# Phi of the first two query tiles of the last quarter, second attention: three operations on ScalarE and one on VectorE in place of one and two

## The chip, the cores and the metric

The kernel runs on one core of a Trainium2 chip. The metric is device time in microseconds (us) of one execution; lower is better. Engines are named as the profile names them: PE is TensorE's matmul, PEld its weight load, DVE is VectorE, ACT is ScalarE, POOL is GpSimd, and SPq is the queue of SyncE, which issues nearly all DMAs. Each engine takes its own instructions strictly in order; an instruction that waits for another engine holds up all that stands behind it on its engine.

## The reference

The network has four layers on x of shape 2048 x 1024: linear attention (A), gated ReGLU block (B), and the same two again with the same weights. What matters here is the attention:

```
qkv = layernorm(x) @ wqkv                       # 32 heads of 32
phi = lambda t: where(t > 0, t + 1, exp(t)) + 1e-6
pq, pk = phi(q), phi(k)
kv  = einsum("bhsd,bhse->bhde", pk, v);   z = sum over s of pk
o   = (pq @ kv) / ((pq . z) + 1e-6)
x   = x + o.reshape(B, S, D) @ wo
```

Phi is computed as max(t, 0) + (min(exp(t), 1) + 1e-6), or, which is the same in value, as max(t, 0) + (exp(-max(-t, 0)) + 1e-6).

## The kernel before

The 2048 rows are 16 tiles of 128 rows; four tiles are a quarter (`sc` or `q`, 0 to 3; `j` is the tile in its quarter). The 1024 columns are two halves of 512 (`c` or `n2`, 0 and 1). A tile's half is a unit: eight matmuls of 128 x 512 into one PSUM bank. `l` is 0 in the first attention and 2 in the second, so `l and ...` is true in the second alone.

An attention layer runs in this order: keys and queries of quarters 0 to 2 in turn (`k_unit`, `q_unit`), the keys of quarter 3, then the product of normalised x and phi(k) (`m_products`, L534), from which `kv` comes (`kv_half`, L485), and then the queries of quarter 3, the output units and the folding of `wo`.

**Queries of quarter 3.** `q_unit(sc, j, c)` projects (`project`, L436) and takes phi of the PSUM bank `ps` into half `c` of tile `pq`. `phi` has two kinds:

```
if kind == "v":
    nc.scalar.activation(out=e, in_=ps, func=ACT.Exp)                          # L375
else:
    nc.scalar.activation(out=e, in_=ps, func=ACT.Relu, scale=-1.0)             # L377
    nc.scalar.activation(out=e, in_=e, func=ACT.Exp, scale=-1.0)               # L378
    nc.scalar.activation(out=e, in_=e, func=ACT.Identity, bias=self.eps6[:, 0:1])   # L379
...
if kind == "v":
    nc.vector.tensor_scalar(out=e, in0=e, scalar1=1.0, scalar2=1e-6, op0=ALU.min, op1=ALU.add)  # L383
nc.vector.scalar_tensor_tensor(out=out, in0=ps, scalar=0.0, in1=e, op0=ALU.max, op1=ALU.add)    # L385
```

Before, queries of quarters 0 to 2 take kind "s", those of quarter 3 kind "v"; keys always take "v". L383 reads and writes float32 in SBUF; L385 reads `ps` from PSUM and `e` from SBUF and is the last reader of the bank.

**Folding.** `finish_kv` copies the two banks of `kv` to SBUF, one with DVE (L588) and one with ACT (L589). `fold_wo(n)`, n = 0 to 3, multiplies 16 small blocks of it by `wo` (PE, L641) into four PSUM banks, of which DVE copies one (L650) and ACT three (L648) into `T`. All four calls use the same four banks (`kv0`, `kv1` of one pool, two of `ps3`), so a fold's first matmul waits until the copies of the fold ahead are done.

**The order on PE** in this stretch of the second attention is: query unit (0,0); the last part of `kv`; units (0,1), (1,0); fold 0; units (1,1), (2,0); fold 1; units (2,1), (3,0); fold 2; unit (3,1), first output unit (L656); fold 3; the other output units, each added to x by DVE (L663).

**Denominators.** For each of the 16 query tiles `z_mult` (POOL, L610) multiplies pq by z into `kvc`, `z_sum` (DVE, L615 to L617) sums and inverts, `z_scale` (POOL, L622) scales pq, and a DMA transpose on SPq (L627) brings it to `pqT`, the operand of the output units. These chains for tiles 0 to 10 are under way while PE computes the last queries.

**What sets the order.** Tasks are put off by a count of units (`later.at`, one tick each unit). In this stretch the orders of DVE and POOL are those in which the program issues (`manual_schedule`), so DVE's queue holds L383 and L385 of the units, L588, L650 and the denominators' L615 to L617 interleaved; the order of ACT is the framework's. SPq issues, in order: transposes of pqT, the two halves of `wo` (L37), x rows 0 to 7 back from DRAM (L230), and the first weights of the next layer (L778, L781).

**After it.** The output units of the later quarters run beside the layer norm of the next layer: DVE statistics (L154, L159), ACT scaling (L188), DMA transposes to xnT (L352), and the sums of xnT on DVE (L823 to L826) which the next layer's first matmuls (L850) read.

Of the kernel before, what the change touches and what calls it, by code (L numbers as in the profile page):

```python
# [15 lines left out]
NW = 512  # L16
# [73 lines left out]
class _Net:  # L90
# [318 lines left out]
    def layer_A(self, l, last_ln):  # L409
# [18 lines left out]
        def project(name, l_q, j, between=None):  # L428
            w = ring.get((l, name))

            spare = l_q < self.NQ - 1 and next(turns) % 3 == 2
            ps = (self.ps3 if spare else self.ps).tile([P, NW], F32, tag="b" if spare else "a")
            for kt in range(KT):
                if between and kt == KT - 2:
                    between()
                nc.tensor.matmul(by_row(ps), lhsT=self.xnT[l, l_q][:, kt, j * P:(j + 1) * P],  # L436
                                 rhs=w[:, kt, :].rearrange("p (b i d) -> p i b d", i=R, d=HD),
                                 start=(kt == 0), stop=(kt == KT - 1))
            return ps
# [153 lines left out]
        def q_unit(sc, j, c, lag=None):  # L593
            if c == 0 and (sc, j) not in pq_of:
                a = self.slot(f"pq{l}_{sc}", [P, QT, D])
                for i in range(QT):
                    pq_of[sc, i] = a[:, i, :]
            pq = pq_of[sc, j]
            self.phi(project(f"q{c}", sc, j), pq[:, c * NW:(c + 1) * NW], "s" if sc < self.NQ - 1 else "v")
            if c == H - 1 and lag is not None:  # L600
                later.at(lag, lambda: z_mult(sc, j))

# [5 lines left out]
        def z_mult(sc, j):  # L608
            prod = ksum
            nc.gpsimd.tensor_tensor(out=prod, in0=pq_of[sc, j], in1=zrow, op=ALU.mult)  # L610
            later.at(2, lambda: z_sum(prod, sc, j))
# [79 lines left out]
        if l == 0:  # L691
            first = self.head_units(lambda *a: k_unit(0, *a), lambda *a: q_unit(0, *a), *steps)
        else:
            first = column_major(k_unit, 0)
# [6 lines left out]
        if l == 0:  # L701
            with self.tc.manual_schedule(engines={mybir.EngineType.DVE, mybir.EngineType.SP,
                                                  mybir.EngineType.Activation}):
                quarter0()
        else:
            run(first, column_major(q_unit, 0))
        for q in range(1, self.NQ - 1):
            if (l, q) == (0, 1):
                for i in range(self.U // 2):
                    later.at(1 + 8 * i, lambda i=i: self.make_d(2 * i))  # L710
            run(row_major(k_unit, q), row_major(q_unit, q))
# [351 lines left out]
```

## Time and profile before

| | us |
|---|---|
| median of 5 runs | 1486.56 |
| lowest to highest | 1484.92 to 1489.65 |
| profiled execution | 1486.11 |
| its span, first to last instruction | 1484.2 |
| PE busy in the span | 1471.7 (99%) |
| DVE busy | 872.9 (59%) |
| ACT busy | 513.1 (35%) |
| POOL busy | 283.8 (19%) |
| PE busy from 893 to 917 us | 20.36 of 24.00 |

The span is read in microseconds from its start. In the timeline a line is start, length, engine, code line, operation, out<-in, with the idle time ahead of it and what ended that in brackets; consecutive instructions of one kind are merged with a count. A matmul's length has its pipeline's tail in it, so that the next may start before its end. In the list of waits a line is who waited for whom: total, times, longest. The last queries of the second attention and the four folds lie between 893 and 917 us; the first matmul of the next layer starts at 972.93 us.

### The profile page before, as it was taken

How to read it: one execution, taken by the hardware profiler on the slowest of the kernel's cores; microseconds unless marked ns; L12 is line 12 of the kernel's file. 1: busy time of each engine (PE TensorE's matmuls, PEld its weight loads, DVE VectorE, ACT ScalarE, POOL GpSimd, SP SyncE). 2: the span in 40 equal slices, each digit the busy share in tenths (PEclk: the TensorE clock that was granted, in tenths of full speed). 3: DMA queues.
4: the chain of work that ended last, by engine and by line, in shares of the span. 5: the costliest groups of instructions: out<-in, count | busy, mean ns of one | idle time of the engine just before them, and what ended most of it. 6: DMA issues, size and time to landing. Idle time of an engine off the chain costs nothing.

```text
span 1484.2 us, 18646 instructions
## 1 busy us (share of the span) xinstructions
PE 1471.7 (99%) x7007; PEld 668.2 (45%) x7007; DVE 872.9 (59%) x1495; ACT 513.1 (35%) x919; POOL 283.8 (19%) x190
## 2 busy tenths in 40 slices
PE   9999999999999999999999999999999999999999
PEld 4444444444444444444444444444444444444444
DVE  8995787666594434455379767873445433434632
ACT  5752323333330333340067423343333203333300
POOL 1356540111100011110023484401111000111000
PEclk9999999999999999999999999999999999999999
DMA  9855438444458954435833029894444688444461
GB/s 280 226 164 175 114 60 245 156 142 157 160 187 252 339 175 132 149 128 195 255 99 71 1 41 291 211 279 142 137 147 131 186 245 269 142 142 147 149 208 43
DMA packets 316059, 251.32 MB, mean 169 GB/s; under 512 B 105536, under 2 KB 291136, under 8 KB 315072
## 3 DMA queue, kind: packets, MB, share of 16 engines
q1 hardware_dynamic: 306000, 229.80, 52.7%
q10 hardware_dynamic: 9968, 20.32, 3.6%
q8 instruction: 55, 0.90, 0.3%
q14 instruction: 36, 0.29, 0.1%
HBM read 190.84 MB, written 34.60 MB: 152 GB/s over the span
## 4 chain that ended last, share of the span: by engine, by line
PE 90%; DVE 6%; POOL 2%; DMA 1%; issue 1%; ACT 0%; SPq 0%; DVEq 0%
PE ps L436 14%; PE yg L850 10%; PE dy L934 10%; PE yu L850 10%; PE dv L934 7%; PE dx L934 7%; PE xu L850 6%; PE xg L850 6%; PE ps L473 4%; PE vg L850 3%; PE vu L850 3%; PE zu L850 3%; PE zg L850 3%; PE ps L656 2%; DVE x L663 1%; DVE stats L154 1%
## 5 line engine op out<-in xcount | busy, mean ns | idle before, releaser
L850 PEld LDWEIGHTS <-w 128*128 128x128 f16 (+1 forms) x3136 | 306.6, 98 | 371.3 <-DVE w L788 1.1
L888 POOL TENSOR_TENSOR h<-m5u,m5g 128x512 f16<-128x512 f32 x56 | 71.1, 1269 | 813.1 <-DVE m5u L884 802.2
L436 PE MATMUL ps<-w,xnT 128*128 128x512 bf16 x1024 | 225.4, 381 | 0.4 <-DMA w<-in_A_wqkv_dram 0.3
L934 PEld LDWEIGHTS <-h 128*128 128x128 f16 x1120 | 109.6, 98 | 132.2
L881 DVE TENSOR_TENSOR zg<-yg,m5g 128x512 f32<-128x512 f32 x56 | 39.2, 699 | 203.5 <-PE yg L850 203.5
L436 PEld LDWEIGHTS <-xnT 128*128 128x128 bf16 x1024 | 99.7, 98 | 121.9 <-issue 3.8
L850 PE MATMUL yg<-s,w 128*128 128x512 f16 x448 | 115.1, 379 | 0.0
L850 PE MATMUL xu<-xnT,w 128*128 128x512 f16 x448 | 115.0, 379 | 0.0
L850 PE MATMUL xg<-xnT,w 128*128 128x512 f16 x448 | 115.0, 379 | 0.0
L850 PE MATMUL yu<-s,w 128*128 128x512 f16 x448 | 115.0, 379 | 0.0
L656 PE MATMUL ps<-T,pqT 128*128 128x512 bf16 x512 | 111.5, 379 | 2.8 <-DVE x L663 2.8
L858 ACT ACTIVATE m5g<-m5g 128x512 f32<-128x512 f32 x56 | 35.2, 629 | 200.2 <-DVE m5g L884 200.2
L934 PE MATMUL dy<-w,h 128*128 128x512 f16 x448 | 98.0, 379 | 0.0
L934 PE MATMUL dx<-w,h 128*128 128x512 bf16 x448 | 97.3, 379 | 0.0
L610 POOL TENSOR_TENSOR kvc<-pq,kvc 128x1024 f32<-128x1024 bf16 x32 | 70.4, 2201 | 72.0 <-DVE den L615 57.8
L656 PEld LDWEIGHTS <-pqT 128*128 128x128 bf16 x512 | 49.9, 98 | 63.5 <-issue 3.8
L154 DVE BATCH_NORM_STATS2 stats<-x 128x6 f32<-128x512 f32 (+1 forms) x120 | 76.5, 672 | 0.7 <-DMA x<-in_A_x_dram 0.4
L161 ACT ACTIVATE rstd<-mv,eps 128x1 f32<-128x1 f32 x64 | 18.1, 289 | 160.9 <-DVE mv L159 160.8
L455 POOL TENSOR_TENSOR kvc<-kvc,slab 128x512 f32<-128x512 f32 x46 | 58.1, 1270 | 74.2 <-DVE slab L385 56.5
L861 DVE TENSOR_TENSOR h<-yu,r 128x512 f16<-128x512 f32 x56 | 38.7, 692 | 56.6 <-PE yu L850 56.6
L884 DVE TENSOR_TENSOR m5u<-yu,m5u 128x512 f32<-128x512 f32 x56 | 38.7, 692 | 54.0 <-PE yu L850 53.0
L934 PEld LDWEIGHTS <-e 128*128 128x128 f16 x448 | 43.8, 98 | 52.9
(127 smaller groups left out, 1971.1 us busy)
## 6 DMA issues: line engine op xcount, KB each, us to landing
w<-in_B_W_gate_dram SPq DMA_DIRECT2D x56, 512.0 KB, 5.8
w<-in_B_W_up_dram SPq DMA_DIRECT2D x56, 512.0 KB, 4.6
w<-td SPq DMA_DIRECT2D x32, 896.0 KB, 4.7
w<-in_B_W_down_dram SPq DMA_DIRECT2D x24, 896.0 KB, 5.5
w<-tg SPq DMA_DIRECT2D x42, 512.0 KB, 6.8
w<-tu SPq DMA_DIRECT2D x42, 512.0 KB, 5.5
w<-in_A_wqkv_dram SPq DMA_DIRECT2D x10, 1024.0 KB, 8.3
away<-x SPq DMA_DIRECT2D x16, 512.0 KB, 4.1
```

Source lines behind the costliest of these rows:

```text
L154: self.nc.vector.bn_stats(out=stats[:, c, :], in_=src[:, c * fmax:(c + 1) * fmax])
L436: nc.tensor.matmul(by_row(ps), lhsT=self.xnT[l, l_q][:, kt, j * P:(j + 1) * P], rhs=w[:, kt, :].rearrange("p (b i d) -> p i b d", i=R, d=H ...
L455: nc.gpsimd.tensor_tensor(out=ksum[:, cols], in0=ksum[:, cols], in1=pk, op=ALU.add)
L473: nc.tensor.matmul(ps, lhsT=self.xn[l, t][:, d * P:(d + 1) * P], rhs=self.pk[l, t][:, h * NW:(h + 1) * NW], start=(t == 0), stop=(t == sel ...
L610: nc.gpsimd.tensor_tensor(out=prod, in0=pq_of[sc, j], in1=zrow, op=ALU.mult)
L656: nc.tensor.matmul(ps, lhsT=pqT[sc][:, g, j * P:(j + 1) * P], rhs=T[g // 4][:, g % 4, n2 * NW:(n2 + 1) * NW], start=(g == 0), stop=(g == G ...
L850: nc.tensor.matmul(ps, lhsT=W[w][m][:, k, :], rhs=A[m][:, k, :], start=start and k == 0, stop=k == 3, skip_group_check=True)
L861: self.last_put = nc.vector.tensor_tensor(out=h[:, b, :], in0=ps, in1=R.pop(b), op=ALU.mult)
L881: nc.vector.tensor_tensor(out=Z[w], in0=Y[w], in1=V[w], op=ALU.add)
L884: nc.vector.tensor_tensor(out=V[w], in0=Y[w], in1=V[w], op=ALU.add)
L888: nc.gpsimd.tensor_tensor(out=h[:, 3, :], in0=V["u"], in1=V["g"], op=ALU.mult)
L934: nc.tensor.matmul(banks[j], lhsT=A(k)[:, j * P:(j + 1) * P], rhs=w[:, i, :], start=start and k == 0, stop=k == self.U - 1, skip_group_che ...
```

## The change

The queries of tiles 0 and 1 of quarter 3 in the second attention, four units in all, take phi of kind "s": L377, L378 and L379 on ACT and L385 on DVE, where they took L375 on ACT and L383 and L385 on DVE. Tiles 2 and 3, the first attention and all keys are as before.

```diff
             pq = pq_of[sc, j]
-            self.phi(project(f"q{c}", sc, j), pq[:, c * NW:(c + 1) * NW], "s" if sc < self.NQ - 1 else "v")
+            self.phi(project(f"q{c}", sc, j), pq[:, c * NW:(c + 1) * NW],
+                     "s" if sc < self.NQ - 1 or (l and j < 2) else "v")
```

The file has one line more from there on, so that the changed kernel's L642, L651 and L657 are L641, L650 and L656 of the kernel before.

## The prediction

> **What bounds the kernel now.** The page comes first: PE is busy for 1471.7 of 1484.2 us, so a change gains only where PE idles or runs slowly.
>
> ```profile
> PE 1471.7 (99%) x7007; PEld 668.2 (45%) x7007; DVE 872.9 (59%) x1495; ACT 513.1 (35%) x919; POOL 283.8 (19%) x190
> ```
>
> Then PE's waits from 893 us to the end:
>
> ```profile
> PE fold L641 <- DVE T L650: 3.1, 1, 3.1
> PE ps L656 <- DVE x L663: 1.7, 1, 1.7
> PE fold L641 <- DVE kvc L588: 0.6, 1, 0.6
> PE vg L850 <- DVE s L823: 0.3, 1, 0.3
> ```
>
> Two of the four end on DVE copies in the stretch that the change touches. PE's timeline there:
>
> ```profile
> 895.84 3.62 PE L436 MATMUL ps<-w,xnT 128*128 128x512 bf16 x16
> 900.05 0.44 PE L641 MATMUL fold<-w,kvc 32*32 32x512 bf16 x16 [0.59 <-DVE kvc L588]
> 900.42 3.63 PE L436 MATMUL ps<-w,xnT 128*128 128x512 bf16 x16
> 907.10 0.44 PE L641 MATMUL fold<-w,kvc 32*32 32x512 bf16 x16 [3.06 <-DVE T L650]
> 907.47 5.31 PE L436 MATMUL ps<-w,xnT 128*128 128x512 bf16 x16
> 912.72 0.43 PE L641 MATMUL fold<-w,kvc 32*32 32x512 bf16 x16
> ```
>
> After the 3.06 us idle the same 16 matmuls take 5.31 instead of 3.63 us. The table of stretches says why (the clock is the third number from the end):
>
> ```profile
> 907.10:908.10 1.00, 1.00 (x19) 1.00 1.11 446
> 908.10:911.50 3.40, 3.40 (x10) 0.52 1.02 408
> 911.50:917.00 5.50, 5.50 (x54) 0.99 1.06 378
> ```
>
> The granted clock halved for 3.4 us. Why the copies were late is in DVE's and POOL's timelines:
>
> ```profile
> 896.57 2.03 DVE L383 TENSOR_SCALAR e<-e 128x512 f32<-128x512 f32 x1
> ...
> 899.31 0.68 DVE L588 CAST kvc<-kv 128x512 bf16<-128x512 f32 x1
> ...
> 901.64 1.97 DVE L383 TENSOR_SCALAR e<-e 128x512 f32<-128x512 f32 x1
> ...
> 904.32 1.34 DVE L383 TENSOR_SCALAR e<-e 128x512 f32<-128x512 f32 x1
> ...
> 906.37 0.68 DVE L650 CAST T<-fold 128x512 bf16<-128x512 f32 x1
> ...
> 908.70 0.36 DVE L383 TENSOR_SCALAR e<-e 128x512 f32<-128x512 f32 x1
> ```
>
> ```profile
> 896.20 2.12 POOL L610 TENSOR_TENSOR kvc<-pq,kvc 128x1024 f32<-128x1024 bf16 x1
> ...
> 901.20 2.13 POOL L610 TENSOR_TENSOR kvc<-pq,kvc 128x1024 f32<-128x1024 bf16 x1 [0.83 <-DVE den L615]
> 903.28 2.09 POOL L622 TENSOR_TENSOR pq<-pq,den 128x1024 bf16<-128x1024 bf16 x1
> 908.92 1.91 POOL L622 TENSOR_TENSOR pq<-pq,den 128x1024 bf16<-128x1024 bf16 x1 [3.55 <-DVE den L617]
> ```
>
> L383 takes 0.36 us while POOL is idle (908.70). Under a POOL operation it ends 0.28 us after that one: 898.60 after 898.32, 903.61 after 903.33, 905.66 after 905.37. So three L383 stretched to 2.03, 1.97 and 1.34 us stand on DVE ahead of L588 and L650.
>
> **What is removed and added.** Four L383 go from DVE: 2.03, 1.97, 1.34 and 0.36 us, 5.70 in all. Four L375 (median 0.578) become L377, L378, L379 (medians 0.597, 0.630, 0.722) on ACT. All 48 of the L379 before took 0.705 to 0.724, POOL busy or not, so ACT's chain is not stretched as L383 is. A chain at 827.88 shows their spacing: 827.88, 828.51, 829.17, next instruction 829.80; another has DVE's L385 starting 0.76 us after L379's start (825.72, 826.48). Exp to L383 to L385 is now Relu, Exp, add to L385. No DMA, matmul or POOL instruction is added or moved. In the changed program ACT's third L379 comes after the first L648 of fold 0.
>
> **The new times**, by the spacings of the rows (ACT first copy L648 0.55 after a fold's start; DVE 0.60 per L385, L588 or L650, 1.24 for L615; fold 0.73 after L650's start; 16 matmuls and change to a fold 3.55; fold 0.37):
> - ACT: L377 at 895.15 as L375 did, L379 at 896.44. DVE: L385 at 897.20 (before 898.70), L588 at 897.81 and done 898.49. PE reaches fold 0 at 895.84 + 3.55 = 899.39 without a wait: it gains 0.66. The first half of wo, issued 893.64 and 5.3 to land, is there at 898.94, the next latest.
> - ACT: second chain 897.83 to 899.75, third 899.75, 900.38, then the copy L648 at 901.01, L379 at 901.50, the other copies until 903.2. DVE: L615 898.41, L617 900.2 (its L616 waits for POOL), L385 at 900.50, the third L385 waits for L379 until 902.26, L650 at 902.87. Fold 1 can start at 903.60; PE is there at 899.39 + 0.37 + 3.55 = 903.31. Idle 0.29 (before 3.06).
> - ACT: fourth chain 903.11 to 905.03, L375 of unit (2,0) at 905.03, copies of fold 1 until 907.1. DVE: L615 903.47, L617 904.93, L385 905.20, and L383 of (2,0) ready at 905.81. But POOL's L622 starts 0.50 after L617 (908.42 and 908.92 before), at 905.43, and runs to 907.34: L383 ends 907.6. L385 907.7, L650 908.31, fold 2 at 909.04. PE is there at 903.60 + 0.37 + 3.55 = 907.52: a new idle of 1.52.
> - Fold 3: DVE's copy of fold 2 is done at 912.3, PE comes at 909.04 + 3.92 = 912.96 (3.92 as before, 912.72 to 916.64). No wait.
>
> **The sum.** Before, PE lost 0.66 + 3.13 at folds 0 and 1 (907.10 less 900.05 + 0.37 + 3.55) and 1.70 to the clock (912.72 less 907.47 + 3.55): 5.49. After: 0.29 + 1.52 = 1.81. Fold 3 moves from 916.64 to 912.96: 3.68 us.
>
> The clock: an idle of 3.06 us halved it; one of 1.72 us at 960.3 did not (clock 1.00 from 960.3 to 966). 1.52 lies below both, so I count no fall after. The Trainium skill, page "TensorE: Matmul & The Clock Gate", section "HAM oscillation — how this bites in real kernels", allows gaps up to about 3.4 us. By that 3.06 should not have throttled; the clock row says it did, and the row decides. Read by the page, the 1.70 is not the change's to win, and the sum is 3.68 - 1.70 = 1.98.
>
> **Bounds.** Unseen before are a POOL operation against the moved L383 of (2,0), and the chain between two copies. If that L383 is not held, the 1.52 goes: 5.20 gained. If it must let the next POOL operation (L610, 2.1) pass too, the idle is about 3.65, the clock falls (1.70), and the sum is 3.68 - 2.13 - 1.70 = -0.15. I take 1.52: at 898.32 DVE got in between two POOL operations that follow each other (POOL's next one lengthened to 2.10).
>
> **Whether it reaches the end.** From 913 us PE runs output units; the next waits are 1.72 and 0.34 us at 962 and 973, behind DVE and the xnT transposes. That work starts from L663 rows released by PE, and SPq's transpose at 931.77 waits for POOL's L622, which follows DVE's L617 of 927.92. The DMA engines rest from 928.5 to 931.7 (share 0.01), so there is room for 3 us without a backlog. I let it all move with PE; what is lost there lies between 0 and 3.68. After 973 PE has no wait.
>
> The span becomes 1484.2 - 3.68 = 1480.5. The profiled execution (1486.11, 1.91 over its span) becomes 1482.4; the median is 0.45 above the profiled one, so 1482.9.
>
> **Rivals.**
> - *The clock term is not in every run* (0.20). One profile shows one fall; an idle of 3.06 is not far above 1.72, which did not cause it. For: the five runs differ by more than 1.7. Against: the row. Gain 3.68 - 1.70 = 1.98: 1484.6.
> - *The transposes hold PE* (0.12): slower than before at its end. For: the chain of waits passes from 956.44 through two of them (3.40 and 4.21 us), DMA share 1.09 to 1.19 from 943 to 960. Against: the rest at 928.5. If half is given back, 1484.8. If they do not move at all, the idle at 962 grows by 3.68 to 5.40 and the clock falls: 1482.9 + 3.68 + 1.70 = 1488.3. It decides against the change once the idle passes some 2.4 to 3.06 and more than 1.98 is given back.
> - *POOL keeps L383 out twice* (0.06): -0.15 above, 1486.7.
> - *L383 of (2,0) is not held* (0.05): 1481.4.
> - *Nothing comes of it* (0.02): ACT, not DVE, releases the folds. Its copies of fold 1 end 1.9 us before DVE's, so it would have to slip by that and 3.68. 1486.6.
>
> **How the numbers follow.** The forecast has 0.55, with its own range 1481.4 to 1483.9. A difference of 0.2%, 2.97 us, is about what a measurement of this kernel can tell from none. Faster: 0.55 + 0.05 = 0.60. Slower: 0.06, from the transposes (0.04) and the double hold (0.02) with some 1.3 us more than priced. Same: the rest, 0.34. The range reaches from the unheld L383 less 0.4 (the median's distance), 1481.0, to half-way into the rivals with no gain, 1486.2; some 0.15 lies outside.
>
> **What would show it.** Four L383 fewer (76); L385 at 897.2; no wait of fold 0 on L588; fold 1 idle under 0.5; fold 2 (L642) idle near 1.5 behind L651; clock 1.00 from 893 to 917; fold 3 near 913; idle at 962 near 1.7. It is wrong if fold 2 idles over 2.5, if the clock still falls, or if the idle near 960 grows.

## The result, and the profile after

The changed kernel takes 1482.51 us (median of 22 runs, 1481.44 to 1486.04), against 1486.46 before (42 runs, 1484.78 to 1490.09). The ratio is 0.9974, 95% interval 0.9968 to 0.9979. The interval lies below 1, so the change makes the kernel faster, by 3.95 us. The forecast was 1482.9, in 1481.0 to 1486.2, faster. The profiled execution has a span of 1480.2 us in place of 1484.2.

PE's waits from 893 us to the end, in the changed kernel (who waited for whom: total, times, longest):

```profile
PE fold L642 <- DVE T L651: 1.5, 1, 1.5
PE ps L657 <- DVE x L664: 1.4, 1, 1.4
```

Of the four waits before, the one of fold 0 on `kv`'s copy and that of the next layer on the sums are gone; the wait of 3.06 us before fold 1 is gone and one of 1.46 stands before fold 2. PE's timeline of the stretch:

```profile
893.85 1.89 PE L436 MATMUL ps<-w,xnT 128*128 128x512 bf16 x8
...
900.02 0.43 PE L642 MATMUL fold<-w,kvc 32*32 32x512 bf16 x16
900.38 3.63 PE L436 MATMUL ps<-w,xnT 128*128 128x512 bf16 x16
904.03 0.44 PE L642 MATMUL fold<-w,kvc 32*32 32x512 bf16 x16
904.40 3.63 PE L436 MATMUL ps<-w,xnT 128*128 128x512 bf16 x16
909.48 0.44 PE L642 MATMUL fold<-w,kvc 32*32 32x512 bf16 x16 [1.46 <-DVE T L651]
...
913.41 0.43 PE L642 MATMUL fold<-w,kvc 32*32 32x512 bf16 x16
```

The 16 matmuls after fold 1 take 3.63 us, not 5.31. The stretches of before, read in the changed kernel (the clock is the third number from the end), show no fall:

```profile
904.00:907.10 3.10, 3.08 (x30) 1.00 0.77 239
907.10:908.10 1.00, 0.93 (x5) 1.00 0.98 393
908.10:911.50 3.40, 2.02 (x24) 1.00 1.02 405
```

On DVE the first copy comes early; the one L383 ahead of the second copy is stretched, under the L623 of POOL that runs from 905.85:

```profile
897.82 0.69 DVE L385 SCALAR_TENSOR_TENSOR pq<-ps,e 128x512 bf16<-128x512 f32 x1 [0.53 <-ACT e L379]
898.43 0.68 DVE L588 CAST kvc<-kv 128x512 bf16<-128x512 f32 x1
...
906.17 1.86 DVE L383 TENSOR_SCALAR e<-e 128x512 f32<-128x512 f32 x1
908.14 0.69 DVE L385 SCALAR_TENSOR_TENSOR pq<-ps,e 128x512 bf16<-128x512 f32 x1
908.75 0.68 DVE L651 CAST T<-fold 128x512 bf16<-128x512 f32 x1
```

```profile
905.85 1.91 POOL L623 TENSOR_TENSOR pq<-pq,den 128x1024 bf16<-128x1024 bf16 x1 [1.07 <-DVE den L618]
```

One profile's time splits at three points of PE's timeline: the start of the first query unit, the start of fold 3, and the start of the next layer's first matmul. The table does this for every run below, each by its own profile; "medians" are of the timed runs, and the ratio is to runs of the kernel before on the same chip.

| kernel | first unit at | unit to fold 3 | fold 3 to next layer | rest | median | ratio (interval) |
|---|---|---|---|---|---|---|
| before | 893.22 | 23.42 | 56.29 | 511.27 | 1486.46 | |
| changed | 893.85 | 19.56 | 55.52 | 511.27 | 1482.51 | 0.9974 (0.9968 to 0.9979) |
| e1 before, GpSimd quiet | 893.85 | 17.94 | 57.35 | 511.26 | 1481.26 | 0.9965 (0.9951 to 0.9978) |
| e2 changed, GpSimd quiet | 894.53 | 18.12 | 55.74 | 511.21 | 1481.46 | 0.9965 (0.9952 to 0.9979) |
| e3 before, a unit twice | 892.75 | 23.28 | 56.88 | 511.29 | 1485.94 | 0.9997 (0.9988 to 1.0006) |
| e4 one tile | 893.72 | 20.18 | 56.03 | 511.27 | 1482.72 | 0.9980 (0.9971 to 0.9990) |
| e5 changed, copies first | 892.58 | 17.94 | 56.72 | 511.26 | 1481.16 | 0.9960 (0.9947 to 0.9972) |
| e6 before, copies first | 893.77 | 21.23 | 56.23 | 511.27 | 1484.43 | 0.9983 (0.9974 to 0.9992) |
| e7 all four tiles | 893.83 | 20.40 | 55.99 | 511.28 | 1483.24 | 0.9971 (0.9960 to 0.9981) |
| e8 five units | 893.30 | 19.22 | 56.21 | 511.27 | 1481.80 | 0.9963 (0.9950 to 0.9976) |
| e9 changed, again | 893.02 | 19.56 | 55.84 | 511.28 | 1482.83 | 0.9975 (0.9966 to 0.9984) |
| e10 as e5, again | 892.19 | 17.94 | 56.87 | 511.20 | 1480.48 | 0.9958 (0.9946 to 0.9971) |

The 4.00 us between the two spans are 3.86 in the stretch and 0.77 behind it, less 0.63 that the changed kernel's profile was late when the stretch began. The second column repeats to the hundredth (e9, e10), while the first scatters over 2.3 us in kernels that are nearly alike up to there: so the second column carries the readings, and differences of less than a microsecond between medians do not.

### The profile page after: what moved, and what is told of

It reads as the page before. It is cut to its first block, busy times and chain, and to the rows that moved or that the text cites. A ratio compares the mean times of both kernels' runs of the same rounds, so it can differ in the third digit from the quotient of the medians.

```text
span 1480.2 us, 18649 instructions
## 1 busy us (share of the span) xinstructions
PE 1469.3 (99%) x7007; PEld 667.4 (45%) x7007; DVE 868.2 (59%) x1491; ACT 517.7 (35%) x927; POOL 283.6 (19%) x190
## 4 chain that ended last, share of the span: by engine, by line
PE 86%; DVE 6%; issue 1%; DMA 1%; ACT 0%; DVEq 0%; ACTq 0%
PE yg L851 10%; PE dy L935 10%; PE yu L851 10%; PE ps L436 7%; PE dv L935 7%; PE dx L935 7%; PE xu L851 6%; PE xg L851 6%; PE ps L473 4%; PE vg L851 3%; PE vu L851 3%; PE zu L851 3%; PE zg L851 3%; PE ps L657 3%; PE my L534 1%; DVE x L664 1%
## 5 line engine op out<-in xcount | busy, mean ns | idle before, releaser
L657 PE MATMUL ps<-T,pqT 128*128 128x512 bf16 x512 | 111.5, 379 | 2.4 <-DVE x L664 2.4
L657 PEld LDWEIGHTS <-pqT 128*128 128x128 bf16 x512 | 49.9, 98 | 63.2 <-issue 3.4
```

Source lines behind the costliest of these rows:

```text
L657: nc.tensor.matmul(ps, lhsT=pqT[sc][:, g, j * P:(j + 1) * P], rhs=T[g // 4][:, g % 4, n2 * NW:(n2 + 1) * NW], start=(g == 0), stop=(g == G ...
```

## The experiments

### Is it the waiting for GpSimd? (e1, e2)

Theory: L383 waits for the POOL operation that is running, and DVE's copies stand behind it. Rival: DVE just has one operation per unit too many. Both kernels leave POOL's operations out of the stretch and keep every DVE instruction. In both kernels, tiles 8 to 11 of the second attention lack the product with z, and tiles 7 to 10 lack the scaling, so that part of their result is not computed.

```diff
-            nc.gpsimd.tensor_tensor(out=prod, in0=pq_of[sc, j], in1=zrow, op=ALU.mult)
+            if not l or not 8 <= sc * QT + j <= 11:
+                nc.gpsimd.tensor_tensor(out=prod, in0=pq_of[sc, j], in1=zrow, op=ALU.mult)
...
-            nc.gpsimd.tensor_tensor(
+            if not l or not 7 <= sc * QT + j <= 10:
+                nc.gpsimd.tensor_tensor(
```

> The kernel before, with GpSimd's work for the tiles that fall into the stretch left out in the second attention: the product with z (L610) of tiles 8 to 11 and the scaling (L622) of tiles 7 to 10, so that those tiles' queries are scaled wrongly. All of VectorE's instructions stay, the four L383 too. Theory (L383 waits for GpSimd's running operation): every L383 takes 0.36 to 0.42 us, no wait before folds 0 to 2, clock 1.00, fold 3 some 5.5 us earlier, time 1481.0. Rival (VectorE simply has too much to do; one instruction fewer per unit is what helped): the wait before fold 1 stays above 1.5 us and less than 2 us are gained, 1484.5 or more.

> The changed kernel with the same GpSimd work left out. Theory: the wait of 1.46 us before fold 2 goes, because the L383 of unit (2,0) is no longer held; time about 1481.0, within 0.8 us of the kernel before without that GpSimd work: the change is worth nothing once GpSimd is quiet. Rival (the change helps by itself): it stays some 3.9 us below the kernel before without GpSimd's work.

Measured: with GpSimd quiet the kernel before takes 1481.26 us and the changed one 1481.46; the stretch is 17.94 and 18.12 us. DVE's timeline of e1, with the same four L383 that took 2.03, 1.97, 1.34 and 0.36 us:

```profile
896.41 0.43 DVE L383 TENSOR_SCALAR e<-e 128x512 f32<-128x512 f32 x1 [1.38 <-ACT e L375]
...
899.96 0.36 DVE L383 TENSOR_SCALAR e<-e 128x512 f32<-128x512 f32 x1
...
901.03 0.42 DVE L383 TENSOR_SCALAR e<-e 128x512 f32<-128x512 f32 x1
...
904.49 0.36 DVE L383 TENSOR_SCALAR e<-e 128x512 f32<-128x512 f32 x1
```

All are 0.36 to 0.43, and no fold waits. The edit takes away a little more than the hold of L383: L615 no longer waits for POOL's product (in the kernel before DVE idled 1.68 us for it, until 894.39), and L616, a small operation of the same kind as L383, takes 0.18 us where it took up to 0.62. The durations of the four L383 are read one by one and do not depend on that. What follows: the change is worth 3.86 us of the stretch beside GpSimd's work and -0.18 without it. The rival is out: DVE has time enough for L383, but not for its waiting.

### Is the clock's fall a cost of its own? (e3)

The prediction's sum before had 1.70 us for the halved clock after the long idle. If that is a cost of its own, work put into the idle should make the kernel faster. The eight matmuls of unit (2,0) are done twice over the same bank.

```diff
-            for kt in range(KT):
+            twice = l and l_q == self.NQ - 1 and j == 2 and name == "q0"
+            for kt in list(range(KT)) * (2 if twice else 1):
```

> The kernel before with the eight matmuls of unit (2,0) in the second attention done twice (the second time over the same bank, same values): TensorE has 1.73 us more to do, in the idle before fold 1. Theory (the idle of 3.06 us brings the clock down, in most runs): idle before fold 1 falls to 1.33, fold 1 at the same time as before, the clock stays 1.00, the 16 matmuls after it take 3.63 in place of 5.31, and the kernel is faster by 1.7 us with more work: 1484.8. Rival (the fall of the clock is chance, or has another cause): time unchanged, 1486.5, or the 5.31 stays.

Measured: ratio 0.9997, no difference. The clock part held and the time part did not. PE in e3:

```profile
906.64 0.44 PE L642 MATMUL fold<-w,kvc 32*32 32x512 bf16 x16 [1.33 <-DVE T L651]
907.01 3.63 PE L437 MATMUL ps<-w,xnT 128*128 128x512 bf16 x16
912.10 0.44 PE L642 MATMUL fold<-w,kvc 32*32 32x512 bf16 x16 [1.46 <-DVE T L651]
```

Fold 1's idle fell to 1.33 as expected and the 16 matmuls ran in 3.63 us, but fold 2 then waited 1.46 us for DVE, where it had not waited at all. From fold 1 to fold 2 it is 5.46 us; before it was 5.62. In the kernel before, then, a DVE wait lay hidden under the slow matmuls. Its trace had said so. This is DVE's copy for fold 2 there:

```profile
911.83 0.68 DVE L650 CAST T<-fold 128x512 bf16<-128x512 f32 x1
```

A fold starts 0.73 after its copy's start, so that 912.56 was the earliest, while the slow clock set 912.72. The L383 ahead of that copy belong to units that PE had computed before fold 1, so that the slow matmuls did not delay it. The clock's own share was 0.16, not 1.70.

That the long idle goes with the fall is seen in the timed executions too. On e3's chip the mean clock of an execution, to three places, is 1.000 in 10 of 11 of e3 and in 6 of 20 of the kernel before.

The executions of the kernel before that were timed beside e1 to e10 also show that the fall cost little. The fall of 3.4 us to 0.52 lowers the mean clock over 1484 us by 0.0011. To three places that mean is 1.000 in 13 of 54 executions and below in 41. On the three chips the medians of those at 1.000 are 1486.32, 1487.04 and 1486.47, and of those at 0.999 they are 1485.91, 1486.94 and 1485.80: an execution with the full clock was no faster than one with 0.999. Six more have 0.996 to 0.998 and took 1486.69 to 1488.47 us, each above the median of its chip; they have no trace, so where their clock fell is not known.

### How much does one tile bring? (e4)

```diff
-                     "s" if sc < self.NQ - 1 or (l and j < 2) else "v")
+                     "s" if sc < self.NQ - 1 or (l and j < 1) else "v")
```

> The changed kernel with the new kind for tile 0 alone (two units). By the same working as in the prediction: third L383 held by L610 until 902.7, fold 1 idle 0.8, the fourth L383 free, fold 2 idle about 1.6, no fall of the clock, fold 3 3.1 us earlier than before: 1483.4. If each unit were worth the same (a quarter each of 3.95), it would be 1484.5.

Measured: stretch 20.18 us, 3.24 less than before (3.1 expected); idle before fold 1 0.63 (0.8), before fold 2 1.46 (1.6); 1482.72 us. DVE in e4:

```profile
901.58 1.48 DVE L383 TENSOR_SCALAR e<-e 128x512 f32<-128x512 f32 x1
...
906.10 0.36 DVE L383 TENSOR_SCALAR e<-e 128x512 f32<-128x512 f32 x1
...
907.18 1.35 DVE L383 TENSOR_SCALAR e<-e 128x512 f32<-128x512 f32 x1
```

The first of the two tiles carries 3.24 of the 3.86 us. It is the one whose two L383 were held longest (2.03 and 1.97 us before); of the second tile the L383 of (1,0) is still held here (1.48) and that of (1,1) is not (0.36). So the gain follows the held L383, though not one for one, and it is not the same for each unit.

### Is the new wait the held L383 of (2,0)? (e5, e6)

Here nothing moves between engines. The joins (L383, L385) of the units that have a fold behind them come one tick later, so that DVE has the copies of folds 0, 1 and 2 ahead of them. e5 does this to the changed kernel, e6 to the kernel before.

```diff
-                return lambda: (u(), fold_wo(i // 2) if i % 2 == 0 else None)
+                def unit():
+                    self.phi_lag = 1 if l and i % 2 == 0 else 0
+                    u()
+                    self.phi_lag = 0
+                    if i % 2 == 0:
+                        fold_wo(i // 2)
+
+                return unit
```

> The changed kernel with VectorE's order altered: in the second attention the joins (L383, L385) of units (1,0), (2,0) and (3,0) and of the first output's neighbour come one tick later, so that the copies of folds 0, 1 and 2 stand ahead of them. Theory (the 1.46 us before fold 2 are the held L383 of (2,0) standing ahead of the copy): no wait before folds 1 and 2, first query unit to fold 3 in 18.0 to 18.4 us (before 23.42, changed 19.56), time some 1.4 us below the changed kernel, 1481.1. Rival (ScalarE's copies are next at once): the wait before fold 2 stays over 1 us, behind ScalarE, and the time is the changed kernel's, 1482.5.

> The kernel before with the same altered order and nothing moved to ScalarE. Theory: fold 0 waits 0.6 as before, fold 1 about 1.1 in place of 3.06 (two held L383 stand ahead of the copy, not three), fold 2 about 1.6 (held L383 of units (1,0) and (1,1)), clock 1.00; first query unit to fold 3 in 21.3 us, time 1484.4: order alone is worth about half of the change. Rival (the order matters as much as the operations taken away): 1482.5.

Measured: e5 has no wait before any fold and a stretch of 17.94 us, the same as with GpSimd quiet; 1481.16 us. DVE in e5:

```profile
904.98 0.68 DVE L651 CAST T<-fold 128x512 bf16<-128x512 f32 x1
905.58 0.68 DVE L383 TENSOR_SCALAR e<-e 128x512 f32<-128x512 f32 x1
...
906.91 1.63 DVE L383 TENSOR_SCALAR e<-e 128x512 f32<-128x512 f32 x1
...
909.25 0.68 DVE L651 CAST T<-fold 128x512 bf16<-128x512 f32 x1
```

The L383 of the next unit is still held (1.63 us), and it costs nothing: the copy behind it starts at 909.25, in time for fold 3 at 910.52. Together with e2, where the order is unchanged, POOL is quiet and the wait is gone too, that shows the cause of the 1.46 us before fold 2: it was the order on DVE together with the hold.

e6 measures 21.23 us (21.3 expected) and 1484.43 (1484.4): order alone shortens the stretch of 23.42 by 2.19. Its waits are not quite those expected: 1.00 before fold 1 (1.1), 0.84 before fold 2 (1.6), and a new one of 0.46 inside the units, where PE waits for the L385 that is now later and frees the bank:

```profile
908.34 1.89 PE L436 MATMUL ps<-w,xnT 128*128 128x512 bf16 x8 [0.46 <-DVE pq L385]
```

### Would more on ScalarE bring more? (e7, e8)

```diff
-                     "s" if sc < self.NQ - 1 or (l and j < 2) else "v")
+                     "s" if sc < self.NQ - 1 or l else "v")                     # e7: all four tiles
+                     "s" if sc < self.NQ - 1 or (l and 2 * j + c < 5) else "v") # e8: five units
```

> The changed kernel with the new kind for all four tiles (eight units, sixteen more operations on ScalarE than before). ScalarE then has some 15.6 us for phi and 5.9 for copies in the stretch. Theory: the L383 of (2,0) is gone but ScalarE's copies of folds 1 to 3 come later behind its chains, so that little is won or lost: first query unit to fold 3 in 19.3 to 20.5 us, a wait before folds 2 and 3 behind ScalarE, time 1482.5 within 0.8. Rival (more of the same gains more): the wait before fold 2 goes, 1481.1.

> The changed kernel with the new kind for unit (2,0) too. The chain on ScalarE ends with L379 at about 1.3 us after where L375 ended, so that L385 of (2,0) starts only some 0.3 us earlier than behind the held L383. Theory: wait before fold 2 about 1.2 in place of 1.46, first query unit to fold 3 in 19.3, time within 0.5 of the changed kernel, 1482.3. Rival: the wait goes as a whole, 1481.1.

Measured: e7 has a stretch of 20.40 us, longer than the changed kernel's 19.56, and 1483.24 us; e8 19.22 and 1481.80. The waits of e7 between 893 and 917 us:

```profile
DVE pq L385 <- ACT e L379: 7.7, 6, 1.6
...
PE fold L642 <- DVE T L651: 2.2, 2, 1.1
```

PE waits for DVE by name, but DVE's L385 waits for ScalarE's L379, six times and 7.7 us in all. As ACT issues each unit's chain and the three copies of a fold in one queue, the hold by GpSimd is exchanged for a queue on ScalarE, and a second wait, of 1.11 us before fold 3, appears. The expectation named ScalarE as the cause, and that is where the chain leads, though PE's own row names DVE. The fifth unit (e8) takes 0.34 us off the wait before fold 2; the medians can't tell it from the changed kernel.

### Side by side: the changed kernel and copies first (e9, e10)

The changed kernel as it is, and e5's kernel again, with no further edit:

```diff
 (e9: as the changed kernel; e10: as e5)
```

> The changed kernel again, on the chip of the next run, for a comparison side by side: ratio to the kernel before 0.9974, first query unit to fold 3 in 19.56 us, wait before fold 2 of 1.46.

> The changed kernel with the copies of the folds ahead of the joins on VectorE, again, beside the changed kernel. Theory: no wait before folds 1 and 2, first query unit to fold 3 in 17.94 us, 1.6 us below the changed kernel less up to 1.1 that the waits behind the transposes before the next layer may give back (1.40 us in all in the changed kernel, 2.49 in the run before of this one): 0.5 to 1.6 us faster than the changed kernel. Rival (what is won in the stretch is given back there as a whole): no difference.

Measured on one chip: the changed kernel 1482.83 us (11 runs, 1480.63 to 1484.90), copies first 1480.48 (5 runs, 1480.04 to 1480.99); ratios to before 0.9975 and 0.9958, whose intervals overlap a little. The medians differ by 2.35 us, more than the 0.5 to 1.6 expected. The profiles explain less: 1.62 won in the stretch and 1.03 given back from fold 3 to the next layer, where PE waits for DVE and the transposes (1.5 us in e9, 1.7 + 1.0 in e10); another 0.83 lies ahead of the stretch, where the two kernels are alike. So copies first has the lowest medians of the kernels tried that compute everything. Against the changed kernel the profiles explain 0.6 us and the medians show more; how much more is not settled. Against e8, whose interval (0.9950 to 0.9976) takes in both ratios of copies first, the timed runs do not decide. What sets the waits behind fold 3 was not tried.

## Why the prediction was right

**The hold of L383** was right, and e1 and e2 show it: without POOL's operations there is neither a loss before nor a gain from the change.

**The times of the changed stretch** were right within 0.2 us each. On the changed profile's own start (0.63 later) the forecast puts fold 0 at 900.02, fold 1 at 904.23, fold 2 at 909.67 and fold 3 at 913.59; measured are 900.02, 904.03, 909.48 and 913.41. Of the idle of 0.29 before fold 1 only 0.1 came: ScalarE's third chain began 0.06 us earlier and ran with spacings of 0.61 and 0.53 us where 0.63 was taken, so that its L379 came at 901.94 and not 902.13. The new idle before fold 2 was given as 1.52 and is 1.46, behind the L383 that was named.

**The sum** was 3.68 and the stretch gave 3.86. The step that failed is inside it: "1.70 to the clock". Fold 2 before was late by 1.70, that is so, but 1.54 of it was DVE's copy, which allowed no start before 912.56 even at full clock (e3). The total did not suffer, since it was taken from the start of fold 3 before and after, and the loss was only put down to the wrong cause. Where it would have done harm is in the rival built on it, *the clock term is not in every run*, priced at a gain of 1.98. Its premise is true (13 of 54 executions have a mean clock of 1.000), but with the clock term at 0.16 the gain would have been 3.52. The rivals that count a new fall at 1.70 went untested, since none came in the changed profile.

The clock row of the kernel before stands on its own: after 3.06 us of idle the clock was at 0.52. The Trainium skill, page "TensorE: Matmul & The Clock Gate", section "HAM oscillation — how this bites in real kernels", allows idle gaps up to about 3.4 us, and this row does not agree with it. The time is no test of that sentence: the sum of 1.98 worked out by it took away 1.70 us of which the clock held only 0.16.

**That it all reaches the end** was right: SPq's transpose of 931.77 came at 928.54, 3.23 earlier as fold 3 did, and the wait at 962 went from 1.72 to 1.40 instead of growing. That this wait fell by 0.32 and that the second wait, 0.34, vanished was not foreseen; 0.77 us in all came behind the stretch. In the profile the 0.63 that the stretch began late takes most of that back, so that the span came so near the forecast (1480.2 for 1480.5) partly by luck.

**The rivals.** Transposes that hold PE: no, by the same rows. POOL keeping L383 out twice: no, L383 ended at 908.03, 0.27 after the first operation's end (907.76). L383 of (2,0) not held: no, 1.86 us. ScalarE as the releaser of the folds: in the changed kernel only for the 0.1 us before fold 1, by way of the L379 that DVE's L385 waited for; in e7, with eight units in place of four, for both waits.

## What to carry to other kernels

Ask of every late copy what stands ahead of it in its engine's queue and whether that instruction is longer than usual: here a 0.36 us operation took up to 2.03, of which its engine's busy share (59%) says nothing and its mean of 0.65 us over 80 instances little. Three ways out were tried here, apart from each other: move the held operation, quieten the one that holds it, or put the copy ahead of it. The last needed no work on any engine. Alone it reached a stretch of 21.23 us, and on top of the change 17.94, the same as with GpSimd quiet.

A loss that ends on one cause may have another right under it. Before a term such as a slow clock is counted as a gain, look for the next releaser of the same instruction and count only the distance to that.

## What the runs showed that was not expected

When the clock falls after an idle is not settled. Idles of 1.72 us (before), 2.35 (e3) and 2.44 (e1, at 955.5 to 957.9) left it at 1.00, and one of 3.06 brought it to 0.52; but of 54 executions of the kernel before, 13 show a mean clock of 1.000. Whether their idle was shorter or the same idle had another effect is not known, since they have no trace.

Of 23 executions of the changed kernel (22 timed and the profiled one) 3 have a mean below 1.000; their median is 1484.69 us against 1482.38 of the others. In e1 to e10 there are 7 such executions, and each lies above the median of its kernel. There a fall goes with a longer time, which between 0.999 and 1.000 in the kernel before it did not. Where in these executions it lies, and whether it is the cause or follows from another wait, is not known, since they have no trace.
